# Batch 0's k in two kinds of load, a held queue, and another place for one product: linear attention into a SwiGLU block

## The chip, the cores and the metric

The kernel runs on one core of a Trainium2 chip. The time is that of the device in microseconds, median of three runs. A core has engines that run side by side: TensorE (PE) multiplies matrices and writes to PSUM, VectorE (DVE) and ScalarE (ACT) work element by element, GpSimd (POOL) and SyncE (SP) here mostly issue transfers (DMA). Each waits for the others by semaphores. In this kernel the instructions of an engine run in the order in which the program states them; nothing reorders them.

## The reference

Eight batches of eight heads, 576 positions, 64 elements a head. Attention without a softmax, its result as tokens into a gated block:

```python
def _attn_ref(q, k, v):
    def phi(x):
        return np.where(x > 0, x, np.exp(x) - 1.0) + 1.0
    q_p, k_p = (phi(q), phi(k))
    kv = np.einsum('bhsd,bhse->bhde', k_p, v)
    z = np.sum(k_p, axis=2)
    num = np.einsum('bhsd,bhde->bhse', q_p, kv)
    den = np.einsum('bhsd,bhd->bhs', q_p, z)[..., None] + 1e-06
    return (num / den).astype(np.float32)

def _moe_ref(x, w_gate, w_val, w_out):      # x: 4608 x 512, w_gate and w_val: 512 x 1536, w_out: 1536 x 512
    g = x @ w_gate
    silu = g * (1.0 / (1.0 + np.exp(-g)))
    val = x @ w_val
    return (silu * val @ w_out).astype(np.float32)
```

Since phi(x) = max(x, 0) + min(exp(x), 1), a phi costs one exp on ScalarE and a maximum, a minimum and an add on VectorE.

## The kernel before

The work goes in nine groups of 512 tokens. For each group, layer 1 is 12 blocks (`l1`, 8 products each), layer 2 is 4 blocks of 12 products. Attention for a batch is prepared while an earlier group is in the layers. Only batch 0 has nothing to hide behind: its attention is the head of the kernel. PSUM is four pairs of tiles (`pp4`), handed out in turn.

Loads: q of batch 0 comes in fp32 on SP's queue; everything else is issued by GpSimd and becomes fp16 on the way.

```python
def ld(src, dst, b, lp):                    # half lp of a batch: 288 KB of fp16
    nc.gpsimd.dma_start(out=dst[b % NB][:, 2 * lp:2 * lp + 2, :], in_=...)

for h in (0, 2):                            # q32 in two halves
    nc.sync.dma_start(out=q32[:, h:h + 2, :], in_=...)
nc.gpsimd.iota(out=idx[:, :], ...)
ld2(k, kr, 0)                               # both halves of k, then of v
ld2(v, vr, 0)
ld_w1(0, 256, 0, 2)                         # w_gate and w_val, by columns and rows
ld_w1(0, 256, 2, 4)
ld_w1(256, 512)
# ... the other columns, batch 1's k and q, w_out, batch 1's v
```

The head of batch 0. `lp` is one half of the heads. `warm` is products whose result nobody reads, to fill TensorE's waits. q is turned by TensorE and gets its phi afterwards (`q_exp` on ScalarE, `q_phi` on VectorE). `zt` sums k's phi over positions, once for the maximum (`kp`) and once for the minimum (`ek`); `zr_copy` takes the sum from PSUM; `t_corners` with `Zr` gives the denominator; `lnrd` its inverse by a logarithm and an exp for each of two tiles; `kv_corner` gives k.v, `r_copy` takes it from PSUM; `t_corners` with `R` gives the numerator; `x_t` multiplies the two into xT, the input of layer 1.

```python
nc.vector.tensor_copy(**q_cast(0))
act(**q_cast(1))
nc.vector.tensor_copy(**q_cast(2))
nc.vector.tensor_copy(**q_cast(3))
warm(WARM[0])
q_one(qa); q_one(qb)
q_turn(0, qa)
q_exp(0, 0, qa); q_exp(0, 1, qa)
warm(WARM[1])
q_turn(1, qb)
q_exp(1, 0, qb)
exp_k(0, 0)
q_exp(1, 1, qb)
warm(WARM[2])
exp_k(0, 1)
q_phi(0, 0, qa); q_phi(0, 1, qa)
mx_k(0, 0)                                  # maximum of k, first half
q_phi(1, 0, qb)
mn_k(0, 0)                                  # minimum of its exp
mx_k(0, 1)
zt(0, 0, X[1], kp, True, False)
warm(WARM[3])
zt(0, 0, X[1], ek, False, True)
zr_copy(0, 0, X[1])
warm(WARM[4])
t_corners(0, Zr, 0, pp4[2])
lnrd(pp4[2], 0)
add_k(0, 0)
mn_k(0, 1)
zt(0, 1, Y[0], kp, True, False)
kv_corner(0, 0, kp, True, True)
r_copy(0, 0, 1, "VV")
zt(0, 1, Y[0], ek, False, True)
zr_copy(0, 1, Y[0])
q_phi(1, 1, qb)
warm(WARM[5], ps=X[0])
t_corners(0, R, 0, X)
x_t(0, 0, X)
kv_corner(0, 1, kp, True, False)
t_corners(0, Zr, 1, Y)
lnrd(Y, 1)
# ... k.v with ek, R, then layer 1 by chunks of xT: l1_mm
```

Batch 1 is prepared in layer 2 of group 0, in two pairs, `dz` and `cq`. `den` writes a denominator into a pair and takes its logarithms, `cq` first. Before, k.v of batch 1 is written over `dz`.

```python
def p1_open():
    b1p["z"] = kvp[1] = pair()
    ring.pop()
    b1p["q"] = pair()
    ring.pop()

# in layer2_0:  cq, dz = b1p["q"], b1p["z"]
def s0():
    exp_q(1, 0); exp_q(1, 1); exp_k(1, 1)
    mx_p(0); mn_q(1, 0); add_p(0)           # phi of q, then of k's second half
    mx_p(1); mn_q(1, 1); add_p(1)
    mn_k(1, 1); add_k(1, 1)
# s1: turn(cq), q of batch 1 turned; s2: position 8 and z
def s4():
    den(1, cq)
    den(0, dz)
    for i in range(4):
        act(rd[i // 2][:, i % 2, :], lnt[i][:, :], AF.Exp, scale=-1.0)
# ...
s4()
for t in range(4):
    if t == 2:
        for lp in range(2):
            kv_corner(1, lp, kp, True, True)
        r_copy(1, 0, 2, "VV")
    if t == 3:
        nx(0, dz)                           # numerator and x_t, into dz, then into cq
        nx(1, cq)
    for fb in range(FO, FB):
        l2_mm(0, t, fb)
    # ...
```

Of the kernel before, what the change touches and what calls it, by code (L numbers as in the profile page):

```python
# [7 lines left out]
FP32 = mybir.dt.float32  # L8
# [5 lines left out]
P = 128  # L14
# [3 lines left out]
def kernel(  # L18
# [10 lines left out]
    nc = tc.nc  # L29

    B, H, S, D = q.shape
# [4 lines left out]
    J = S // C  # L36
# [3 lines left out]
    EPS = 1e-6  # L40
    SC = 4096.0
    NB = 3
    WARM = (4, 2, 5, 4, 2, 1)

    sb = ctx.enter_context(tc.tile_pool(name="sb", bufs=1))
    pp = ctx.enter_context(tc.tile_pool(name="ps", bufs=1, space=bass.MemoryType.PSUM))
# [2 lines left out]
    def many(shape, dt, name, n=2):  # L49
        return [sb.tile(shape, dt, name=f"{name}_{i}") for i in range(n)]  # L50

    kr = many([P, HL, J * D], FP16, "kr", NB)
    qr = many([P, HL, J * D], FP16, "qr", NB)
    vr = many([P, HL, J * D], FP16, "vr", NB)
    ek = many([P, 2, J, 2 * D], FP16, "ek")
    eq = many([P, HL, J * D], FP16, "eq")
    kp = many([P, 2, J, 2 * D], FP16, "kp")
    qp = many([P, 2, J, 2 * D], FP16, "qp")
    qT = many([P, 2, J, 2, C], FP16, "qT")
    R = many([P, 2, 2, D], FP16, "R", 3)  # L60
# [2 lines left out]
    rd = many([P, 2, 512], FP16, "rd")  # L63

    q32 = sb.tile([P, HL, J * D], FP32, name="q32")
    lnt = many([P, 512], FP32, "lnt", 4)
    prod = sb.tile([P, J, 2 * D], FP16, name="prod")
    den = sb.tile([P, 2, J * 2], FP32, name="den")
# [16 lines left out]
    gate = sb.tile([P, 1], FP16, name="gate")  # L85
# [7 lines left out]
    def pair(p=None):  # L93
        i = 0 if p is None else [x is p for x in ring].index(True)
        p = ring.pop(i)
        ring.append(p)
        return p
# [4 lines left out]
    def ld(src, dst, b, lp):  # L102
        nc.gpsimd.dma_start(out=dst[b % NB][:, 2 * lp:2 * lp + 2, :],  # L103
                            in_=src[b].rearrange("(l a) (c j) d -> (a c) l (j d)", a=2, j=J)[:, 2 * lp:2 * lp + 2, :])

    def ld2(src, dst, b):
        ld(src, dst, b, 0)
        ld(src, dst, b, 1)

    def ld_w1(f0, f1, c0=0, c1=4):  # L110
        for (src, dst) in ((moe_w_gate, wg), (moe_w_val, wv)):
            nc.gpsimd.dma_start(out=dst[:, c0:c1, f0:f1],
                                in_=src[P * c0:P * c1, f0:f1].rearrange("(c p) f -> p c f", p=P))

    def ld_w2(f0, f1):
        nc.gpsimd.dma_start(out=wo[:, f0:f1, :],
                            in_=moe_w_out[P * f0:P * f1, :].rearrange("(c p) f -> p c f", p=P))

    def act(out, in_, func=AF.Copy, scale=1.0, bias=0.0):
        nc.scalar.activation(out=out, in_=in_, func=func, bias=bias, scale=scale)  # L120

    def warm(n, w=512, ps=None):
        for _ in range(n):
            nc.tensor.matmul(out=(ps or pp4[1][1])[:, 512 - w:512], lhsT=ones[:, :],  # L124
                             rhs=ones[:, 0:1].to_broadcast([P, w]), start=True, stop=True)

    def hs(lp):
        return slice(2 * lp, 2 * lp + 2)

    def jl(t, b, lp):  # L130
        return t[b % 2][:, lp, :, :].rearrange("p j (l d) -> p l j d", d=D)

    def lj(t, b, lp):
        return t[b % NB][:, hs(lp), :].rearrange("p l (j d) -> p l j d", d=D)

    def exp_k(b, lp):
        act(jl(ek, b, lp), lj(kr, b, lp), AF.Exp)
# [4 lines left out]
    def mx_k(b, lp):  # L142
        nc.vector.tensor_scalar(out=jl(kp, b, lp), in0=lj(kr, b, lp), scalar1=0.0, scalar2=None, op0=ALU.max)  # L143

    def mn_k(b, lp):
        a = ek[b % 2][:, lp, :, :]
        nc.vector.tensor_scalar(out=a, in0=a, scalar1=1.0, scalar2=None, op0=ALU.min)  # L147
# [29 lines left out]
    kvp = {}  # L177
# [17 lines left out]
    def r_copy(b, l0, l1, engs):  # L195
        for hh in range(2):
            src = kvp[b][hh][:, D * l0:D * l1].rearrange("p (l d) -> p l d", d=D)
            if engs[hh] == "A":
                act(R[b % 3][:, l0:l1, hh, :], src)
            else:  # L200
                nc.vector.tensor_copy(out=R[b % 3][:, l0:l1, hh, :], in_=src)  # L201
# [42 lines left out]
    def units(g):  # L244
        us = seq[U * g:U * g + U]
        res = []
        for i, (b, j) in enumerate(us):
            if res and res[-1][0] == b and res[-1][2] == j:
                res[-1][2] = j + 1
            else:  # L250
                res.append([b, j, j + 1, C * i])
        return us, res
# [3 lines left out]
    def corners(ps, W, b, lp, j0, j1, c0):  # L256
        for l2 in range(2):
            rows = slice(D * l2, D * l2 + D)
            for hh in range(2):
                nc.tensor.matmul(out=ps[l2][C * hh:C * hh + C, c0:c0 + C * (j1 - j0)],  # L260
                                 lhsT=W[rows, lp, hh, :], rhs=qt(b, lp, hh, j0, j1)[rows],
                                 start=True, stop=True)
# [75 lines left out]

    for h in (0, 2):
        nc.sync.dma_start(out=q32[:, h:h + 2, :],
                          in_=q[0].rearrange("(l a) (c j) d -> (a c) l (j d)", a=2, j=J)[:, h:h + 2, :])
    nc.gpsimd.iota(out=idx[:, :], pattern=[[-1, P]], base=0, channel_multiplier=1)
    ld2(k, kr, 0)
    ld2(v, vr, 0)
    ld_w1(0, 256, 0, 2)
    ld_w1(0, 256, 2, 4)
    ld_w1(256, 512)
    ld_w1(512, 768)  # L350
    ld_w1(768, 1024)
    ld(k, kr, 1, 0)
    ld_w1(1024, 1280)
    ld_w1(1280, 1536)
    ld(k, kr, 1, 1)
    ld_w2(0, 4)
    ld(q, qr, 1, 0)
    ld_w2(4, 5)
    ld(q, qr, 1, 1)
    ld_w2(5, 6)  # L360
    ld_w2(6, 8)
    ld_w2(8, 12)
    ld2(v, vr, 1)

    nc.scalar.preload_act_table_set("natural_log_exp_and_others")
    nc.vector.memset(ones[:, :], 1.0)
# [53 lines left out]
    def zt(b, lp, ps, t, first, last):  # L420
        for j in range(J):
            nc.tensor.matmul(out=ps[:, 0:2], lhsT=t[b % 2][:, lp, j, :], rhs=ob[:, 0:P:C],  # L422
                             start=(first and j == 0), stop=(last and j == J - 1))

    def zr_copy(b, lp, ps):
        nc.vector.tensor_scalar(out=Zr[b][:, lp, :, :], in0=ps[:, 0:2].unsqueeze(2).to_broadcast([P, 2, D]),
                                scalar1=1.0 / SC, scalar2=None, op0=ALU.mult)
# [13 lines left out]
    def t_corners(g, W, lp, ps):  # L441
        for (b, j0, j1, c0) in units(g)[1]:
            corners(ps, W[b], b, lp, j0, j1, c0)

    def q_one(pair_):
        for h in range(2):
            nc.tensor.matmul(out=pair_[h][:, :], lhsT=part[:, :], rhs=ones[:, 0:1].to_broadcast([P, 512]),
                             start=True, stop=False)

    def q_turn(lp, pair_):  # L450
        for j in range(J - 1):
            nc.tensor.matmul(out=pair_[j // 4][:, P * (j % 4):P * (j % 4) + P],
                             lhsT=qp[0][:, lp, j, :], rhs=id16[:, :],
                             start=False, stop=(j % 4 == 3))

    def q_half(lp, h):
        return qT[0][:, lp, 4 * h:4 * h + 4, :, :].rearrange("p j h c -> p (j h c)")

    def q_exp(lp, h, pair_):
        act(q_half(lp, h), pair_[h][:, :], AF.Exp, bias=m1[:, 0:1])  # L460

    def q_phi(lp, h, pair_):
        a = q_half(lp, h)
        nc.vector.scalar_tensor_tensor(out=a, in0=pair_[h][:, :], scalar=1.0, in1=a, op0=ALU.max, op1=ALU.min)  # L464

    kvp[0] = pp4[1]
    X = [pp4[0][0], pp4[3][0]]
    Y = [pp4[3][1], pp4[0][1]]
    qa, qb = pp4[2], pp4[0]

    def q_cast(h):
        return dict(out=qp[0][:, h // 2, 0:8, D * (h % 2):D * (h % 2) + D],
                    in_=q32[:, h, 0:8 * D].rearrange("p (j d) -> p j d", d=D))

    nc.vector.tensor_copy(**q_cast(0))
    act(**q_cast(1))
    nc.vector.tensor_copy(**q_cast(2))
    nc.vector.tensor_copy(**q_cast(3))
    warm(WARM[0])
    q_one(qa)  # L480
# [3 lines left out]
    q_exp(0, 1, qa)  # L484
    warm(WARM[1])
    q_turn(1, qb)
    q_exp(1, 0, qb)
    exp_k(0, 0)
    q_exp(1, 1, qb)
    warm(WARM[2])  # L490
    exp_k(0, 1)
    q_phi(0, 0, qa)
    q_phi(0, 1, qa)
    mx_k(0, 0)
    q_phi(1, 0, qb)
    mn_k(0, 0)
    mx_k(0, 1)
    zt(0, 0, X[1], kp, True, False)
    warm(WARM[3])
    zt(0, 0, X[1], ek, False, True)  # L500
    zr_copy(0, 0, X[1])
    warm(WARM[4])
    t_corners(0, Zr, 0, pp4[2])
    lnrd(pp4[2], 0)
    add_k(0, 0)
    mn_k(0, 1)
    zt(0, 1, Y[0], kp, True, False)
    kv_corner(0, 0, kp, True, True)
    r_copy(0, 0, 1, "VV")
    zt(0, 1, Y[0], ek, False, True)  # L510
    zr_copy(0, 1, Y[0])
    q_phi(1, 1, qb)
    warm(WARM[5], ps=X[0])
    t_corners(0, R, 0, X)
    x_t(0, 0, X)
    kv_corner(0, 1, kp, True, False)
    t_corners(0, Zr, 1, Y)
# [22 lines left out]
    b1p = {}  # L540

    def p1_open():
        b1p["z"] = kvp[1] = pair()
        ring.pop()
        b1p["q"] = pair()
        ring.pop()

    def p1_z():
# [240 lines left out]
```

## Time and profile before

| what | value |
|---|---|
| time, median of 3 | 312.38 us (312.25 to 312.63) |
| span of the profiled run | 310.9 us |
| TensorE busy | 305.7 us (98%) |
| VectorE busy | 204.6 us (66%) |
| ScalarE busy | 153.1 us (49%) |
| GpSimd's queue: moved, share of 16 engines | 18.29 MB, 37.7% |
| SP's queue: moved, share of 16 engines | 13.96 MB, 18.8% |
| time from issue to landing, k in GpSimd's queue (median of 16) | 8.7 us |

Busy time is the sum of an engine's instructions, and TensorE's includes the warming products. A line of a timeline gives start and duration in microseconds, the engine, the line of the program, the operation, what it writes and reads, the shape, and in brackets how long the engine was idle before and what ended that. In the chain of waits each piece is what the next one waited for, followed back from the end. MB of a casting load are counted in what it writes.

### The profile page before, as it was taken

The numbers are of one execution on the slowest core, as the hardware profiler recorded it, in microseconds if no ns is written. First come the engines' busy times: TensorE is split into PE (matmuls) and PEld (weight loads), VectorE is DVE, ScalarE is ACT, GpSimd is POOL, SyncE is SP. The second block draws the span as 40 slices with busy tenths as digits, with TensorE's granted clock in tenths as the row PEclk, the third lists the DMA queues.
The fourth block names the chain that finished last, engine by engine and source line by source line (L and its number), as shares of the span: only waits on it lengthen the run. The fifth ranks groups of instructions, "written<-read, shape, count | busy, mean of one in ns | idle before, by whom it ended". The sixth has DMA issues, their size and how long they took to land.

```text
span 310.9 us, 5597 instructions
## 1 busy us (share of the span) xinstructions
PE 305.7 (98%) x2222; PEld 142.7 (46%) x2222; DVE 204.6 (66%) x361; ACT 153.1 (49%) x231; POOL 48.7 (16%) x74
## 2 busy tenths in 40 slices
PE   8999999999999999999999999999999999999996
PEld 3444444444544454445444544444444444444443
DVE  4755878999599667977697849874991343234320
ACT  4965868539733845365535743475331333133311
POOL 8664444410000410032000500000000000000000
PEclk9999999999999999999999999999999999999999
DMA  8999999999512594229712890314022400140014
GB/s 216 196 197 199 205 206 236 235 206 148 113 27 39 87 188 129 40 41 175 188 28 51 119 244 3 76 36 103 0 51 60 101 1 1 36 100 1 2 33 101
DMA packets 41162, 32.80 MB, mean 106 GB/s; under 512 B 16560, under 2 KB 36144, under 8 KB 41136
## 3 DMA queue, kind: packets, MB, share of 16 engines
q0 software_dynamic: 20496, 18.29, 37.7%
q1 hardware_dynamic: 20496, 13.96, 18.8%
q8 instruction: 17, 0.28, 0.4%
q10 hardware_dynamic: 144, 0.20, 0.2%
q14 instruction: 9, 0.07, 0.1%
HBM read 37.75 MB, written 9.44 MB: 152 GB/s over the span
## 4 chain that ended last, share of the span: by engine, by line
PE 95%; DMA 2%; DVE 1%; ACT 1%; issue 0%; POOL 0%; POOLq 0%; ACTq 0%
PE pp L298 58%; PE pp L305 30%; PE pp L282 2%; DMA kr<-in_k_dram 2%; PE pp L260 2%; PE pp L185 2%; ACT lnt L120 1%; PE pp L124 0%; PE pp L422 0%; PE pp L212 0%; DVE qT L464 0%; PE pp L384 0%; DVE kp L143 0%; DVE R L201 0%; DVE osb L328 0%
## 5 line engine op out<-in xcount | busy, mean ns | idle before, releaser
L120 ACT ACTIVATE sil<-pp 128x512 f16<-128x512 f32 x108 | 63.4, 597 | 100.8 <-PE pp L298 98.0
L298 PE MATMUL pp<-xT,wg 128*128 128x512 f16 x416 | 106.8, 379 | 0.0
L298 PE MATMUL pp<-xT,wv 128*128 128x512 f16 x416 | 106.8, 379 | 0.0
L291 DVE SCALAR_TENSOR_TENSOR hT<-pp,sil 128x512 f16<-128x512 f32 x108 | 72.4, 681 | 48.0 <-PE pp L298 35.3
L305 PE MATMUL pp<-wo,hT 128*128 128x512 f16 (+2 forms) x444 | 97.0, 374 | 0.0
L305 PEld LDWEIGHTS <-hT 128*128 128x128 f16 x444 | 41.9, 98 | 48.7 <-issue 0.8
L298 PEld LDWEIGHTS <-wv 128*128 128x128 f16 x416 | 40.7, 98 | 49.1
L298 PEld LDWEIGHTS <-wg 128*128 128x128 f16 x416 | 40.7, 98 | 48.4
L328 DVE TENSOR_SCALAR osb<-pp 128x512 f32<-128x512 f32 (+1 forms) x19 | 12.6, 667 | 31.9 <-PE pp L305 27.5
L120 ACT ACTIVATE osb<-pp 128x512 f32<-128x512 f32 (+1 forms) x18 | 10.5, 586 | 33.3 <-PE pp L305 33.3
L120 ACT ACTIVATE ek<-kr 128x1152 f16<-128x1152 f16 x16 | 17.9, 1156 | 0.5 <-DMA kr<-in_k_dram 0.4
L120 ACT ACT_TABLE_LOAD x13 | 16.7, 1283 | 2.3 <-PE pp L298 2.1
L719 POOL COPY gate<-qT 128x1 f16<-128x1 f16 x4 | 1.3, 314 | 96.6 <-DMA qT<-qp 96.6
L120 ACT ACTIVATE eq<-qr 128x1152 f16<-128x1152 f16 x14 | 15.7, 1152 | 1.3 <-DMA qr<-in_q_dram 1.3
L229 DVE TENSOR_TENSOR qp<-qp,rden 128x1152 f16<-128x1152 f16 x12 | 16.2, 1347 | 0.0
L220 DVE TENSOR_REDUCE den<-prod 128x18 f32<-128x1152 f16 x12 | 16.1, 1342 | 0.0
L277 DVE TENSOR_SCALAR xT<-pp 128x512 f16<-128x512 f32 (+1 forms) x14 | 8.8, 668 | 6.7 <-PE pp L260 6.7
L103 POOL DMA_DIRECT2D vr<-in_v_dram x16 | 11.7, 729 | 9.8 <-DMA wo<-in_moe_w_out_dram 4.1
L103 POOL DMA_DIRECT2D kr<-in_k_dram x16 | 11.6, 723 | 6.2 <-ACT lnt L120 1.0
L159 DVE TENSOR_TENSOR kp<-ek,kp 128x1152 f16<-128x1152 f16 x15 | 11.4, 758 | 0.5
L147 DVE TENSOR_SCALAR ek<-ek 128x1152 f16<-128x1152 f16 x16 | 7.7, 482 | 5.1 <-ACT ek L120 5.0
L103 POOL DMA_DIRECT2D qr<-in_q_dram x14 | 10.2, 727 | 5.3 <-DMA qr<-in_q_dram 2.7
(86 smaller groups left out, 181.6 us busy)
## 6 DMA issues: line engine op xcount, KB each, us to landing
out_dram<-osb SPq DMA_DIRECT2D x70, 128.0 KB, 2.9
kr<-in_k_dram POOLq DMA_DIRECT2D x16, 288.0 KB, 8.7
vr<-in_v_dram POOLq DMA_DIRECT2D x16, 288.0 KB, 10.0
qr<-in_q_dram POOLq DMA_DIRECT2D x14, 288.0 KB, 11.5
wg<-in_moe_w_gate_dram POOLq DMA_DIRECT2D x5, 256.0 KB, 8.6
wv<-in_moe_w_val_dram POOLq DMA_DIRECT2D x5, 256.0 KB, 9.2
q<-in_q_dram SPq DMA_DIRECT2D x2, 576.0 KB, 4.0
wo<-in_moe_w_out_dram POOLq DMA_DIRECT2D x2, 512.0 KB, 11.9
```

The costliest lines, as they stand in the source:

```text
L103: nc.gpsimd.dma_start(out=dst[b % NB][:, 2 * lp:2 * lp + 2, :], in_=src[b].rearrange("(l a) (c j) d -> (a c) l (j d)", a=2, j=J)[:, 2 * lp ...
L120: nc.scalar.activation(out=out, in_=in_, func=func, bias=bias, scale=scale)
L147: nc.vector.tensor_scalar(out=a, in0=a, scalar1=1.0, scalar2=None, op0=ALU.min)
L159: nc.vector.tensor_tensor(out=a, in0=ek[b % 2][:, lp, :, :], in1=a, op=ALU.add)
L185: nc.tensor.matmul(out=ps[hh][D * l2:D * l2 + D, D * lp:D * lp + D], lhsT=t[b % 2][rows, lp, j, D * l2:D * l2 + D], rhs=vr[b % NB][rows, 2 ...
L220: nc.vector.tensor_reduce(out=den[:, c, :], in_=prod[:, :, :].rearrange("p j (l d) -> p (j l) d", d=D), axis=AX.X, op=ALU.add)
L229: nc.vector.tensor_tensor(out=qv, in0=qv, in1=rden[:, c, :].unsqueeze(2).to_broadcast([P, 2 * J, D]), op=ALU.mult)
L277: nc.vector.tensor_scalar(out=dst, in0=ps[l2][:, c0:], scalar1=1.0 / SC, scalar2=None, op0=ALU.mult)
L291: nc.vector.scalar_tensor_tensor(out=hT[g % 2][:, fb, :], in0=ps[1][:, :], scalar=SC, in1=s[:, :], op0=ALU.mult, op1=ALU.mult)
L298: nc.tensor.matmul(out=ps[h][:, :], lhsT=w[:, c, P * fb:P * fb + P], rhs=xT[g % 2][:, c, :], start=(c == 0), stop=(c == 3))
L305: nc.tensor.matmul(out=l2p[(g, t)][:, n0:n1], lhsT=hT[g % 2][:, fb, P * t:P * t + P], rhs=wo[:, fb, n0:n1], start=(fb == 0), stop=(fb == F ...
L328: nc.vector.tensor_scalar(out=o[:, n0:n1], in0=ps[:, n0:n1], scalar1=1.0 / SC, scalar2=None, op0=ALU.mult)
```

## The change

The first half of batch 0's k goes to SP's queue as fp32, behind q, so that it comes ahead of everything that GpSimd loads; exp and maximum of that half read the fp32 tile. GpSimd's queue starts only when q's first half is cast, by a copy of one element of the result, so that its transfers don't compete with q's. To state that copy after the cast, the block of helpers moves up in the text; the helpers are the same. The order of the head is redone for the new arrivals, and the numbers of warming products with it. And k.v of batch 1 goes into the pair `cq`, whose logarithms come first, in place of `dz`.

```diff
-    WARM = (4, 2, 5, 4, 2, 1)
+    WARM = (4, 2, 6, 1, 2, 1)
+    k32 = sb.tile([P, 2, J * D], FP32, name="k32")
     def lj(t, b, lp):
-        return t[b % NB][:, hs(lp), :].rearrange("p l (j d) -> p l j d", d=D)
+        src = k32 if t is kr and b == 0 and lp == 0 else t[b % NB][:, hs(lp), :]
+        return src[:, :, :].rearrange("p l (j d) -> p l j d", d=D)
-    for h in (0, 2):
-        nc.sync.dma_start(out=q32[:, h:h + 2, :], in_=q[0]...)
+    for (src, dst, h) in ((q, q32, 0), (q, q32, 2), (k, k32, 0)):
+        nc.sync.dma_start(out=dst[:, h:h + 2, :], in_=src[0]...)
     nc.gpsimd.iota(out=idx[:, :], ...)
-    ld2(k, kr, 0)
     # ... constants, helpers (moved up)
+    nc.vector.tensor_copy(**q_cast(0))
+    nc.gpsimd.tensor_copy(out=gate[:, :], in_=qp[0][:, 0, 7, 0:1])
+    ld(k, kr, 0, 1)
     ld2(v, vr, 0)
     # ... all other loads, as before
     q_turn(1, qb)
+    exp_k(0, 0)
     q_exp(1, 0, qb)
-    exp_k(0, 0)
     q_exp(1, 1, qb)
     # ...
     mx_k(0, 0)
+    mn_k(0, 0)
     q_phi(1, 0, qb)
-    mn_k(0, 0)
-    mx_k(0, 1)
     # ... zt, zr_copy, t_corners, lnrd of the first half
     add_k(0, 0)
-    mn_k(0, 1)
-    zt(0, 1, Y[0], kp, True, False)
+    mx_k(0, 1)
     kv_corner(0, 0, kp, True, True)
     r_copy(0, 0, 1, "VV")
+    mn_k(0, 1)
+    q_phi(1, 1, qb)
+    zt(0, 1, Y[0], kp, True, False)
+    warm(WARM[5], ps=X[0])
+    t_corners(0, R, 0, X)
     zt(0, 1, Y[0], ek, False, True)
     zr_copy(0, 1, Y[0])
-    q_phi(1, 1, qb)
-    warm(WARM[5], ps=X[0])
-    t_corners(0, R, 0, X)
     x_t(0, 0, X)
     # ...
-        b1p["z"] = kvp[1] = pair()
+        b1p["z"] = pair()
         ring.pop()
-        b1p["q"] = pair()
+        b1p["q"] = kvp[1] = pair()
```

More of the change, by code (lines that the diff above doesn't have):

```diff
@@ L337, in l2_out @@
         return o
-    for h in (0, 2):
-        nc.sync.dma_start(out=q32[:, h:h + 2, :],
-                          in_=q[0].rearrange("(l a) (c j) d -> (a c) l (j d)", a=2, j=J)[:, h:h + 2, :])
+    for (src, dst, h) in ((q, q32, 0), (q, q32, 2), (k, k32, 0)):
+        nc.sync.dma_start(out=dst[:, h:h + 2, :],
+                          in_=src[0].rearrange("(l a) (c j) d -> (a c) l (j d)", a=2, j=J)[:, h:h + 2, :])
     nc.gpsimd.iota(out=idx[:, :], pattern=[[-1, P]], base=0, channel_multiplier=1)
-    ld2(k, kr, 0)
[L346 to L363, printed above, removed]
     nc.scalar.preload_act_table_set("natural_log_exp_and_others")
@@ L475 @@
     nc.vector.tensor_copy(**q_cast(0))
+    nc.gpsimd.tensor_copy(out=gate[:, :], in_=qp[0][:, 0, 7, 0:1])
+    ld(k, kr, 0, 1)
+    ld2(v, vr, 0)
+    ld_w1(0, 256, 0, 2)
+    ld_w1(0, 256, 2, 4)
+    ld_w1(256, 512)
+    ld_w1(512, 768)
+    ld_w1(768, 1024)
+    ld(k, kr, 1, 0)
+    ld_w1(1024, 1280)
+    ld_w1(1280, 1536)
+    ld(k, kr, 1, 1)
+    ld_w2(0, 4)
+    ld(q, qr, 1, 0)
+    ld_w2(4, 5)
+    ld(q, qr, 1, 1)
+    ld_w2(5, 6)
+    ld_w2(6, 8)
+    ld_w2(8, 12)
+    ld2(v, vr, 1)
     act(**q_cast(1))
```

## The prediction

> **What bounds the kernel now.** I read four views of the profile of before, in this order: the chain of waits for where the end comes from; the timeline where that chain leaves TensorE; the DMA view of the first 20 us; and the times to landing of single transfers.
>
> The chain of waits (start, duration, what):
>
> ```profile
> 1.35 6.95 DMA kr<-in_k_dram
> ...
> 8.32 0.47 DVE kp L143
> ...
> 18.12 17.27 PE pp L298 x80
> 35.38 5.18 PE pp L305 x24
> ...
> 44.43 1.85 ACT lnt L120 x3
> ...
> 46.32 0.79 PE pp L185 x71
> ```
>
> From 18.12 us on, the chain is TensorE work piece after piece, with one break: at 44.43 to 46.27 us it runs over ScalarE's logarithms. Everything that the change touches lies before 53 us; the other 258 us are matrix products it doesn't alter. So the change can only move two things: the head (0 to 18 us), which starts with k's first half landing at 8.30, and that break.
>
> The timeline around both (start, duration, engine, line, what):
>
> ```profile
> 1.35 1.54 POOL L103 DMA_DIRECT2D kr<-in_k_dram  x2 [0.29 <-issue]
> ...
> 4.34 0.43 DVE L475 CAST qp<-q 128x512 f16<-128x512 f32 x1 [2.37 <-DMA q<-in_q_dram]
> ...
> 8.32 0.46 DVE L143 TENSOR_SCALAR kp<-kr 128x1152 f16<-128x1152 f16 x1 [0.42 <-DMA kr<-in_k_dram]
> ...
> 9.96 1.15 ACT L120 ACTIVATE ek<-kr 128x1152 f16<-128x1152 f16 x1
> ...
> 13.11 1.45 DVE L435 SCALAR_TENSOR_TENSOR xT<-pp,rd 128x512 f16<-128x512 f32 x2
> ...
> 38.12 1.17 ACT L120 ACTIVATE eq<-qr 128x1152 f16<-128x1152 f16 x1 [0.48 <-DMA qr<-in_q_dram]
> ...
> 43.39 0.64 PE L260 MATMUL pp<-qT,Zr 64*64 64x64 f16 x16
> ...
> 45.79 0.21 PE L185 MATMUL pp<-vr,kp 64*64 64x64 f16 x1
> ...
> 46.32 0.79 PE L185 MATMUL pp<-vr,kp 64*64 64x64 f16 x71 [0.32 <-ACT lnt L120]
> ```
>
> The reader is to see three things. K is issued at 1.35 and used at 8.32. Batch 1's exp of q at 38.12 waited for a transfer. And k.v of batch 1 began at 45.79, stopped, and went on at 46.32.
>
> The DMA view of the first 20 us (GB/s in 40 slices of 0.5 us):
>
> ```profile
> GB/s 0 0 0 46 180 378 419 396 406 389 270 191 194 194 198 194 194 207 207 198 212 198 168 183 183 188 194 193 198 198 220 188 185 191 202 191 197 199 194 197
> ...
> q0 software_dynamic: 4518, 2.87, 99.0%
> q1 hardware_dynamic: 544, 1.18, 16.3%
> ```
>
> SP's fp32 load of q moves at some 400 GB/s; then GpSimd's casting loads move at some 195, counted in fp16 bytes, which is 390 GB/s of fp32 read. There is no gap from 2.5 us on, and the same view of 20 to 50 us stays near 205. The loads are one saturated stream until past 50 us, so every landing in it is a sum of bytes ahead of it, and a hole anywhere shifts all that follow. From the issues' times to landing: q's halves land at 4.33 and 5.79, k's at 8.30 and 9.74, v's at 11.2 and 12.65, first wv part at 13.97 (first used 14.15), second wv block 18.1 (used 18.82), batch 1's second half of q at 38.1 (used 38.12).
>
> [...] counting packets by queue, GpSimd's k, issued at 1.35, moves its first packet at 4.8, just as SP's q runs out (q's last packets are at 5.3). [...] After the idle spells of before I count 1.3 us to the first packet, and 2.1 to 2.3 us to the full rate (issues at 105.02, 137.78 and 171.28). [...] 1152 fp16 elements in 0.46 us, 512 fp32 ones in 0.43.
>
> **The change, part by part.**
>
> 1. The first half of k in fp32 on SP's queue. It follows q's 1.18 MB directly: 0.59 MB at 400 GB/s is 1.47 us, so its data ends at 5.3 + 1.47 = 6.8. Q's second half landed 0.5 us after its last packet (5.3 to 5.79), so k lands at 7.25 in place of 8.30: 1.05 us earlier.
>
> 2. Its first use. The maximum of k reads fp32. [...] VectorE has two q_phi before it (6.63 to 7.9), so it runs 7.9 to 8.65. Exp of k goes ahead of q's exp, at 7.25 to 8.4 (before 8.32 to 9.48). The min follows at 8.65 to 9.1 (9.52 to 9.98 before). But now q_phi(1,0) stands between the min and the copy of z, and ends only at 9.75 (q's exp, moved back, ends 9.05). So the copy of z starts near 9.8, not 10.46: of 1.05 us some 0.65 are left.
>
> 3. GpSimd's queue waits for q's first cast, ending 4.34 + 0.43 = 4.77. In the later periods the gate copy's start and the next issue are 0.54 us apart (104.48 and 105.02), so the first issue is at about 5.35, 4 us later than now. One transfer of 0.3 MB fp16 less is ahead in that queue. The first landing after an idle spell came 4.0 to 4.4 us after its issue (288 KB, same three places). So k's second half lands at 9.4 to 9.8: as before or slightly earlier. V's first half should follow at 11.0 to 11.4, against 11.2.
>
> 4. The stream. It reaches its full rate about 2.1 us after the issue, at 7.45; SP's data ends at 6.8. The hole is 0.65 us, less some 0.1 us worth of packets in the ramp[...]. Check by sums: before, GpSimd's stream flows from 5.05; after, from 7.45 but with one transfer less (1.53 us at 0.19 MB/us): 7.45 - 1.53 - 5.05 = 0.87. I take 0.7 us later for every landing from the weights on.
>
> 5. The rest of the head. The new order puts the maximum and minimum of k's second half, the copies of R and q_phi(1,1) ahead of the first xT product. From the z copy at 9.8: add to 10.6, maximum to 11.0; k.v waits for v (11.0 to 11.4) and takes 0.45; copies of R to 12.0; min 0.45, q_phi 0.6, z copy 0.25: xT starts at about 13.3, against 13.11. If v lands by 10.8 it is 12.8. So the 0.65 us mostly end in the wait for v; and the first product needs wv, due at 13.97 + 0.3 to 0.7. I expect the start of layer 1 within 0.4 us of now, either way.
>
> 6. Further on. Layer 1 of group 0 has 0.7 us to spare at its second wv block, 1.3 later; the shift of 0.7 just fits. Batch 1's q has nothing to spare: its exp waits for the landing, and the chain exp, min, add, transposes, copies, den ends in the products at 43.39, which TensorE reaches with 0.1 us to spare. So whatever the head gains is lost by 43.4, and the lateness of the stream shows: +0.6 us.
>
> 7. K.v of batch 1 goes to the pair whose logarithms are the first two of four, done by 45.05, before TensorE gets there at 45.8. The stretch from 45.79 to 47.10 (1.31 us) shrinks to the 0.78 us of 72 products: -0.53 us. The R copies then end before the products that need them; v of batch 1 lands at 45.5, or 46.2 if late, and its second half is needed 0.36 us into the work. Later, the exp of batch 2's q is bound by its landing (52.3), but the pair that waits for Silu behind it has 0.95 us to spare, and VectorE, full from 55 to 80, has some 0.5 us: the gain reaches the end.
>
> 8. Two warming products fewer (18 to 16), 0.21 us each, all in time when TensorE waits: nothing.
>
> Sum: +0.6 - 0.53, near +0.1; with the hole at half of that, -0.25.
>
> **Rivals.**
>
> Rival A, the head's gain reaches the end: the stream has no hole[...], and landings after 14 us are unchanged. For it: the author's own order, which expects v early. Against: the exp at 38.12 waits for its landing even now. It would give -0.5 from the break and at most -0.2 from the head: 311.6 to 311.9.
>
> Rival B, the first GpSimd transfer takes its 3.4 us to the first packet (1.35 to 4.8 before) whether or not SP's queue is busy: flow from 8.8, stream later by 2 us. Then the first wv is 1.8 us late and the head with it: +1.3 to +1.6, 313.7 to 314.0. For it: the number of the start itself. Against: the first packet came just as q ran out, and 1.3 us elsewhere.
>
> Rival C, k.v's new place only trades waits: the second pair's product now waits on R's copies. Against: those copies feed both products anyway. It would take away the 0.5: 312.9.
>
> **Range and chances.** My own sum is +0.1, rival A -0.6, rival B +1.4. Weighted 5 to 4 to 2 this is near +0.1; a change tuned by order speaks a little for A, so I say 312.3, 8 in 10 within 311.2 to 313.8. All of these are within 2% (6.2 us) of 312.38: faster 0.01, same 0.98, slower 0.01.
>
> **What would show it.** The fp32 k lands near 7.25 and the maximum takes about 0.76. GpSimd's first load is issued near 5.35, with the DMA row dipping between 6.8 and 7.5. Batch 1's exp of q starts at 38.5 to 39.0. The products at 43.39 come later, and k.v of batch 1 runs without a stop. I am wrong if the stream doesn't dip (A), or dips for over 1.5 us (B), or if layer 1 starts over 0.5 us earlier and keeps that past 43 us.

## The result, and the profile after

| | median | runs | lowest to highest |
|---|---|---|---|
| before | 312.49 us | 6 | 312.25 to 312.67 |
| after | 313.87 us | 6 | 313.65 to 315.32 |

The ratio is 1.0058, with a 95% interval of 1.0035 to 1.0081. The kernel became 1.4 us slower: outside the predicted range by 0.07 us, and on the side that I thought the less likely. The prediction's sum was +0.1.

The chain of waits of the kernel after, cut at 50 us (start, duration, what):

```profile
4.34 0.44 DVE qp L458
...
4.83 0.19 POOL gate L459
5.02 0.76 POOL kr L104
5.78 6.20 DMA vr<-in_v_dram
...
12.02 0.67 PE pp L187 x30
...
21.32 17.27 PE pp L300 x80
38.59 5.18 PE pp L307 x24
...
47.23 1.83 PE pp L307 x8
49.06 0.73 PE pp L187 x72
```

Before, the chain of the head started with k's issue and went over phi of k. Now the cast of q releases the queue, the queue loads v, and v's landing at 11.98 releases TensorE. K, for which the change was made, is not in the chain at all. The block of 80 products of layer 1 starts at 21.32 and took its 17.27 us before as well, but from 18.12. So 3.2 us are lost by 21 us, and the break at 44 us is gone: k.v is one piece of 72.

The timeline of after (start, duration, engine, line, what, and the idle time before it):

```profile
4.34 0.43 DVE L458 CAST qp<-q 128x512 f16<-128x512 f32 x1 [2.36 <-DMA q<-in_q_dram]
...
4.95 0.83 POOL L104 DMA_DIRECT2D kr<-in_k_dram  x1
...
8.03 0.76 DVE L145 TENSOR_SCALAR kp<-k 128x1152 f16<-128x1152 f32 x1
...
9.23 0.72 DVE L149 TENSOR_SCALAR ek<-ek 128x1152 f16<-128x1152 f16 x1 [0.43 <-ACT ek L121]
...
10.46 0.27 DVE L409 TENSOR_SCALAR Zr<-pp 128x128 f16<-128x128 f32 x1
...
12.02 0.67 PE L187 MATMUL pp<-vr,kp 64*64 64x64 f16 x36 [0.82 <-DMA vr<-in_v_dram]
...
15.85 0.61 PE L284 MATMUL pp<-xT,wg 128*128 128x512 f16 x1
...
39.67 2.22 ACT L121 ACTIVATE eq<-qr 128x1152 f16<-128x1152 f16 x2
...
48.99 0.80 PE L187 MATMUL pp<-vr,kp 64*64 64x64 f16 x72
```

and three lines of before to set beside it:

```profile
9.52 0.46 DVE L147 TENSOR_SCALAR ek<-ek 128x1152 f16<-128x1152 f16 x1
...
10.46 0.29 DVE L426 TENSOR_SCALAR Zr<-pp 128x128 f16<-128x128 f32 x1
...
11.47 0.48 PE L185 MATMUL pp<-vr,kp 64*64 64x64 f16 x36
```

Three things are to be seen. The copy of z starts at 10.46, which is exactly when it started before: nothing is left of the earlier k by then. The 36 products of k.v wait 0.82 us for v and take 0.67 us, not 0.48, and one product of 512 columns takes 0.61 us, where it took 0.38 to 0.39. TensorE has half its clock there, as the windows below show. And batch 1's two exps of q no longer wait for a landing; they are two in a row, because the layers themselves come later.

The DMA view of the first 20 us of after, in slices of 0.5 us:

```profile
GB/s 0 0 0 55 198 378 406 392 429 378 323 336 369 256 157 171 164 175 175 161 131 171 173 172 192 158 173 178 188 193 193 195 217 187 191 194 200 194 194 201
...
q0 software_dynamic: 3730, 2.32, 84.9%
q1 hardware_dynamic: 816, 1.77, 25.0%
```

The hole that I expected at 6.8 to 7.5 is not there. Counted by queue, GpSimd's first packet moves at 6.6 us, and SP's last one of k only at 7.7: in the three slices from 6.5 to 8.0 us SP moves 198, 65 and 14 GB/s, and GpSimd 58, 92 and 157. But from 7.0 us on the row does not come back to the 195 of before. It stays between 131 and 192 until about 14 us.

The same stretch of after by windows (length, busy time of PE, PEld, DVE, ACT and POOL with the numbers of instructions, granted clock, DMA share, GB/s):

```profile
6.00:8.00 2.00, 1.37 (x13) 0.84 (x13) 1.94 (x4) 0.82 (x2) 2.00 (x4) 1.00 0.99 238
8.00:10.00 2.00, 1.36 (x14) 0.45 (x13) 1.53 (x3) 1.97 (x3) 2.00 (x3) 1.00 1.20 169
10.00:12.00 2.00, 1.20 (x15) 0.56 (x16) 1.77 (x4) 1.82 (x3) 2.00 (x3) 1.00 1.06 162
12.00:14.00 2.00, 1.98 (x51) 1.04 (x51) 1.27 (x4) 1.94 (x4) 1.16 (x3) 0.52 1.33 175
14.00:16.00 2.00, 2.00 (x90) 1.65 (x87) 1.58 (x5) 0.70 (x2) 1.72 (x3) 0.50 1.44 192
16.00:18.00 2.00, 2.00 (x8) 0.44 (x6) 0.32 (x2) 1.94 (x4) 1.62 (x3) 0.50 1.45 197
```

and before:

```profile
6.00:8.00 2.00, 2.00 (x15) 0.85 (x14) 1.90 (x4) 1.62 (x3) 1.17 (x2) 1.00 1.18 195
8.00:10.00 2.00, 1.64 (x16) 0.55 (x13) 1.54 (x4) 1.68 (x3) 0.76 (x1) 1.00 1.20 202
10.00:12.00 2.00, 2.00 (x66) 1.26 (x66) 1.67 (x4) 1.83 (x4) 1.30 (x2) 1.00 1.29 190
```

TensorE is busy 1.37, 1.36 and 1.20 of each 2 us, where it was 2.00, 1.64 and 2.00. After that its granted clock is 0.52 and 0.50 for six microseconds. This doesn't happen in every run, and the profiled run is one of the longer ones (315.24 us in time). The table puts all 24 runs of the changed kernel, the six of the result and the 18 of the first experiment, by the mean clock that each run was granted:

| mean granted clock of the run | runs | median time |
|---|---|---|
| 1.000 | 5 | 313.56 us |
| 0.995 | 12 | 314.24 us |
| 0.988 or 0.989 | 7 | 315.56 us |

So there are two losses. One is there at full clock: 313.56 us is about 1 us over before. The other is a clock that falls, in some runs more than in others. The experiments had to say which part of the change makes each.

### The profile page after: what moved, and what is told of

Same layout as the page of the kernel before. It is cut to its first block, busy times and chain, and to the rows that moved or that the text cites. A ratio compares the mean times of both kernels' runs of the same rounds, so it can differ in the third digit from the quotient of the medians.

```text
span 313.5 us, 5592 instructions
## 1 busy us (share of the span) xinstructions
PE 306.9 (98%) x2220; PEld 142.7 (46%) x2220; DVE 204.8 (65%) x361; ACT 152.9 (49%) x231; POOL 48.4 (15%) x74
## 4 chain that ended last, share of the span: by engine, by line
PE 95%; DMA 3%; POOL 0%; DVE 0%; issue 0%
PE pp L300 57%; PE pp L307 30%; PE pp L284 3%; PE pp L262 2%; PE pp L187 2%; DMA vr<-in_v_dram 2%; DMA q<-in_q_dram 1%; POOL kr L104 0%; PE pp L405 0%; PE pp L214 0%; PE pp L367 0%; PE pp L125 0%; DVE qp L458 0%; DVE osb L330 0%; PE pp L556 0%; PE pp L385 0%
## 5 line engine op out<-in xcount | busy, mean ns | idle before, releaser
L121 ACT ACTIVATE osb<-pp 128x512 f32<-128x512 f32 (+1 forms) x18 | 10.5, 586 | 33.3 <-PE pp L307 33.3
L121 ACT ACTIVATE ek<-kr 128x1152 f16<-128x1152 f16 x15 | 16.8, 1156 | 0.2 <-DMA kr<-in_k_dram 0.2
L104 POOL DMA_DIRECT2D kr<-in_k_dram x15 | 10.8, 722 | 7.2 <-ACT sil L121 1.9
L161 DVE TENSOR_TENSOR kp<-ek,kp 128x1152 f16<-128x1152 f16 x15 | 11.4, 757 | 0.5
```

Source lines behind the costliest of these rows:

```text
L161: nc.vector.tensor_tensor(out=a, in0=ek[b % 2][:, lp, :, :], in1=a, op=ALU.add)
```

## The experiments

Ratios are against runs of the kernel before on the same chip, with their 95% intervals. None of the kernels leaves work out. The edits are to the kernel before or after, as each says.

### The changed kernel again, and k.v's place alone

The first is the changed kernel itself. The second is the kernel before with only the new place of k.v:

```diff
-        b1p["z"] = kvp[1] = pair()
+        b1p["z"] = pair()
         ring.pop()
-        b1p["q"] = pair()
+        b1p["q"] = kvp[1] = pair()
```

> The changed kernel as it is, for a second trace. In the first trace TensorE's granted clock was 0.5 from about 12 to 18 us (512 columns took 0.61 to 0.63 us, not 0.38), while four of the six timed runs had 0.995 to 1.0. If the lower clock is only an addition that some runs have, a run at clock 1.0 is still about 1.0 us of span above before (311.9 to 312.1 against 310.9), with v's first half landing near 12.0 and the start of layer 1 about 1.6 us later than before. If the lower clock is the whole cause, such a run would be at 310.9.

> The kernel before with one part of the change: batch 1's k.v goes into the pair whose logarithms come first. Theory: the stop in k.v at 45.79 to 46.32 goes, -0.5 us, 311.9 to 312.0. Rival (a trade of waits: the numerator's second pair then waits on the copies of R): no gain, 312.4 to 312.5.

The changed kernel again: 314.56 us, ratio 1.0062 (1.0041 to 1.0083), 18 runs. K.v's place alone: 312.04 us, ratio 0.9981 (0.9967 to 0.9996), 22 runs, the best time of any kernel in this study. From its chain of waits:

```profile
17.60 17.27 PE pp L298 x80
...
43.51 1.83 PE pp L305 x8
45.34 0.73 PE pp L185 x72
```

The 72 products run in one go, straight after layer 2's eight. This part of the change is a gain by itself, and everything else in it together costs 314.56 - 312.04 = 2.5 us.

### More warming products in the changed kernel

```diff
-    WARM = (4, 2, 6, 1, 2, 1)
+    WARM = (4, 2, 8, 3, 2, 1)
     # ... and ahead of k.v of batch 0's first half:
+    warm(4)
     kv_corner(0, 0, kp, True, True)
```

> The changed kernel with eight more warming products, all where TensorE waits in the trace: 8 for 6 before k's sum, 3 for 1 between its two parts, 4 new ones ahead of the first k.v. Theory (the clock falls where TensorE is idle over 6 to 12 us): no run with a clock under 0.995, the two slowest of six runs (315.3) don't come again, and the median is that of the changed kernel at full clock, 313.7 to 313.9. Rival (the lower clock has nothing to do with the waits): some runs at 315.3 as before. If the added products delay k.v, up to +0.3 us.

313.93 us, ratio 1.0045 (1.0029 to 1.0062), 22 runs, of which 21 have a mean clock of 0.999 or 1.000. By windows:

```profile
8.00:10.00 2.00, 2.00 (x18) 0.79 (x16) 1.40 (x3) 1.83 (x3) 2.00 (x3) 1.00 1.14 172
10.00:12.00 2.00, 1.94 (x20) 0.78 (x19) 1.90 (x5) 2.00 (x3) 2.00 (x3) 1.00 1.08 133
```

Products that nobody reads fill the waits, and the clock stays at 1.00. So in this kernel the fall of the clock comes from TensorE's waits (21 of 22 runs kept it, against 5 of 24 of after), and 314.56 - 313.93 = 0.6 us of the loss with it. (The median is still 0.4 us over the 313.56 of the changed kernel's own runs at full clock; no run shows why.) The rest stays: the stream is as slow as in after, 133 GB/s in its worst window. In this run it also reaches batch 1. In its chain of waits:

```profile
29.38 11.21 DMA qr<-in_q_dram
40.59 0.02 issue
40.61 1.17 ACT eq L121
```

Q of batch 1 lands at 40.59, 2.5 us later than the 38.1 of before, and the exp waits for it.

### The hold taken away, and shortened

Is it the hold of GpSimd's queue that makes v late? The first kernel is after without the gate's copy; the second lets the gate copy a constant that is ready at about 2 us, not q's cast.

```diff
-    nc.gpsimd.tensor_copy(out=gate[:, :], in_=qp[0][:, 0, 7, 0:1])     # first kernel: removed
+    nc.gpsimd.tensor_copy(out=gate[:, :], in_=ob[:, 127:128])          # second kernel
```

> The changed kernel without the copy that holds GpSimd's queue; nothing else. Theory (the held queue): GpSimd's first load is issued near 1.3 us again, its data follows SP's without a hole and at 190 GB/s or more from 7 to 12 us (160 to 175 with the gate), v's first half lands by 11.3 and not at 12.0, and the time falls by 1.0 us or more, to 311.9 to 312.8. Rival 1 (the loss is k's half in fp32 behind q and the new order on VectorE): within 0.3 us of the changed kernel, 313.5 to 314.1. Rival 2 (the gate was needed[...]): q's second half and k land over 0.5 us later than with the gate, and the time is 314 or more.

> The changed kernel, but GpSimd's queue is held only until VectorE's last memset (about 2.0 us, so its first load is issued near 2.2 us), just after SP has issued k (1.75 us), and not until q's first cast (4.8 us). Theory (transfers are served in the order in which they were issued, and the changed kernel loses by starting late): k in fp32 lands by 8.0, GpSimd's data follows without a hole at 190 GB/s, v's first half lands by 11.3, and the time is 311.5 to 312.5. Rival[...]: k in fp32 lands near 10, as without any hold (10.2), and the time is 315.5 or more.

No hold: 316.49 us, 1.0113 (1.0068 to 1.0158). Short hold: 314.93 us, 1.0081 (1.0063 to 1.0098). My theory fell: without the hold the kernel is slower still, though v's first half lands at about 11.0 us again (11.98 in after). So the hold is what makes v late; what goes wrong without it is k. The timeline of the kernel without it:

```profile
1.35 0.83 POOL L104 DMA_DIRECT2D kr<-in_k_dram  x1 [0.29 <-issue]
...
10.24 0.76 DVE L145 TENSOR_SCALAR kp<-k 128x1152 f16<-128x1152 f32 x1 [2.33 <-DMA k<-in_k_dram]
```

The fp32 half of k, issued at 1.75, lands at 10.21 without a hold, and the maximum of k at 10.24 waits for it; with the short hold it lands at 9.48, against about 8.0 in after. GpSimd's first packets move at 5.0 and 6.0, while SP's queue still has k to send, and from then on both queues move data side by side: without the hold SP moves 78 to 230 GB/s and GpSimd 83 to 147 in the slices from 5.5 to 8 us. The hold is what makes the fp32 k early. For q it does nothing that can be seen: the cast of its second half starts at 5.72 without the hold, at 5.80 in after and at 5.80 in before. Part of what these two kernels lose is again the clock: all six runs without a hold are at 0.989. But a low share of busy time does not make it fall in every run. The traced run with the short hold kept a full clock, though TensorE was busy less than in after:

```profile
6.00:8.00 2.00, 1.19 (x13) 0.79 (x13) 1.99 (x4) 0.69 (x2) 2.00 (x3) 1.00 1.08 254
8.00:10.00 2.00, 0.78 (x4) 0.17 (x2) 0.49 (x1) 0.49 (x1) 0.08 (x2) 1.00 1.17 215
10.00:12.00 2.00, 1.41 (x21) 0.68 (x21) 1.45 (x4) 2.00 (x4) 1.30 (x2) 1.00 1.23 203
```

### The hold alone, and the new loads in the old order

The hold on the old loads: both halves of k stay fp16 on GpSimd's queue, which is held until q's first cast; order and warming are those of before, and k.v has its new place. Beside it, the new loads and the hold, with order and warming of before. The first edit is to the kernel before with k.v in its new place, the second to the kernel after:

```diff
+    nc.gpsimd.tensor_copy(out=gate[:, :], in_=qp[0][:, 0, 7, 0:1])     # hold alone: after q's first cast,
+    ld2(k, kr, 0)                                                      # all of GpSimd's loads behind it
```

```diff
-    WARM = (4, 2, 6, 1, 2, 1)
+    WARM = (4, 2, 5, 4, 2, 1)                                          # new loads, old order:
     # ... exp_k, mn_k, mx_k, zt, zr_copy and q_phi of the head where they stood before
```

> The kernel before with k.v in its new place (312.04) and, of the loads, only the hold: both halves of k still come by GpSimd's queue, all of which waits for q's first cast. Old order. Theory (the hold is what costs): no data from 5.3 to about 6.6, then a slow stream of 160 to 175 GB/s until about 12 us, k's first half lands near 10.5, 2.2 us later than before; the time is 314.5 to 316. Rival (the slow stream comes from mixing k in fp32 with GpSimd's data): a hole of 1.5 us but then 190 GB/s and more, and 313.3 to 313.8.

> The changed kernel's loads and hold and k.v's new place, with the order and the warming products of before. Theory (the loads do it): as the changed kernel, 313.5 to 314.6, with the clock seldom under 0.995 since there are three more warming products between the parts of k's sum. Rival (the order does it): 312.0 to 312.6.

Hold alone: 315.22 us, 1.0088 (1.0074 to 1.0102). New loads in the old order: 313.53 us, 1.0033 (1.0021 to 1.0045), all five runs at full clock. The DMA view of the hold alone:

```profile
GB/s 0 0 0 51 147 396 373 415 415 396 166 0 12 85 191 196 194 210 187 141 99 138 175 182 171 171 184 181 176 184 193 195 194 196 219 180 197 194 196 199
```

SP's data ends at 5.3 us, and with nothing behind it the hole is open: 166, 0, 12, 85. The stream then comes to 190 and more for two microseconds and falls to 99 at 10 us. There is no fp32 k in this kernel, so the slow stretch is not from mixing with it. The chain of waits of the new loads in the old order:

```profile
6.45 7.42 DMA vr<-in_v_dram
13.87 0.04 issue
13.91 0.48 PE pp L187 x36
...
19.16 17.27 PE pp L300 x80
```

V's second half lands at 13.87 (12.65 before) and releases TensorE, and the 80 products start 19.16 - 17.60 = 1.56 us later than with k.v's place alone, at full clock. (Against the 18.12 of before it is 1.0: the head differs by half a microsecond from trace to trace.) In time it is 313.53 - 312.04 = 1.5 us. That is the cost of the new loads with their hold, without any fall of the clock. The hold alone costs 315.22 - 312.04 = 3.2, in four of its five runs with a clock of 0.995, though it has the order and the 18 warming products of before; the one run at full clock took 314.26, which makes it 2.2. The fp32 k fills the hole and gives back 0.7 of that at full clock (against that one run), and 1.7 between the medians.

The lateness can be read from the packets themselves. I take the time at which GpSimd's queue has moved as many bytes as before (and count the half of k that went to SP's queue as moved). At 14.5 us of before, after is 1.3 us late, its repeat 1.6, the new loads in the old order 1.5, and the hold alone 2.4; without a hold the queue is on time within 0.1. From there to 45 us these numbers stay the same within 0.1. So the prediction was right that a delay in this stream is passed on to all that follows, and the delays of the two kernels with the order of before, 1.5 and 2.4, are near what they lose at full clock, 1.5 and 2.2.

### The new order with the old loads, and fewer warming products

The new order and its warming on the old loads; the same with the warming of before; and k.v's place alone with two warming products fewer than before. All three have k.v in its new place. (The recorded expectation of the third counts three products fewer; its edit takes out two.)

```diff
-    WARM = (4, 2, 5, 4, 2, 1)
+    WARM = (4, 2, 6, 1, 2, 1)     # with the new order;  (4, 2, 5, 4, 2, 1) with it: the second
+    WARM = (4, 2, 4, 3, 2, 1)     # the third, in the old order
```

> New order, new numbers of warming products and k.v in its new place, but the loads of before: k by GpSimd's queue, nothing held. Theory (the order costs little by itself; the loads do it): 312.0 to 312.6 at full clock. Rival (the order costs: one more phi of q before the copy of z, and k's second minimum behind R): 312.8 to 313.5.

> New order and k.v's new place with the loads of before, as in the earlier run of the new order (312.29, where 3 of 21 runs had a clock of 0.988 to 0.995), but with the 18 warming products of before (four, not one, between the two parts of k's sum). Theory (the fewer warming products let the clock fall): no run under 0.998, median 312.0 to 312.3. Rival (the order lets it fall): again one run in seven or more under 0.996.

> The kernel before with k.v in its new place (312.04 by itself) and three warming products fewer (4 for 5, 3 for 4, 1 for 2), since in that kernel's chain of waits the warming products stand right before the sums of k. If they hold the head up: 311.5 to 311.9. If they are what keeps the clock at full: some runs with a clock of 0.988 to 0.995 and a median of 312.1 to 312.8.

New order with its warming: 312.29 us, 1.0000 (0.9987 to 1.0012). With the old warming: 312.37 us, 0.9993 (0.9986 to 0.9999). Old order, fewer warming products: 312.16 us, 0.9986 (0.9979 to 0.9994). On the old loads the order costs at most a few tenths: the medians are 0.2 and 0.3 us over that of k.v's place alone, and the intervals overlap. In the clock, with the new warming 3 of 21 runs fell to 0.995 or 0.988 (313.47, 313.55 and 315.35 us), with the old warming none of 21 fell below 0.998. Three against none is too few to call the warming products the cause. The third kernel, whose clock never went below 0.999, shows the other side: on the old loads and in the old order, two products fewer do no harm.

### What makes the stream slow

Two kernels on the slow stretch itself. The first puts a second hold into after: GpSimd issues k's second half and v, and the weights only after the minimum of k's first half. If issuing while data moves slows the data, the stream should be fast during the pause. The second has the old loads and order, k.v in its new place, and a hold to about 2 us: a later start that leaves no gap behind q.

```diff
     ld2(v, vr, 0)
     # ... after the minimum of k's first half:
+    nc.gpsimd.tensor_copy(out=gate[:, :], in_=ek[0][:, 0, 0, 0:1])
+    ld_w1(0, 256, 0, 2)           # and all that follows
```

```diff
+    nc.gpsimd.tensor_copy(out=gate[:, :], in_=ob[:, 127:128])
     ld2(k, kr, 0)                 # and all that follows
```

> The changed kernel with a second hold on GpSimd's queue: after k's second half and v are issued (to about 7.2 us), the weights wait for the minimum of k's first half (about 9.9 us). So between 7.2 and 10 us data moves while GpSimd issues nothing. Theory (issuing while the data moves is what slows the stream: 160 to 170 in place of 190 to 200 GB/s at 8 to 12 us): 190 GB/s or more from 8 to 10 us, few packets over 0.25 us there, v's first half lands by 11.4. Rival (the slow stretch has to do with starting late or with the data themselves): 145 to 175 GB/s from 8 to 10 us as in the changed kernel, v near 12. The time isn't what is asked: the weights come later still, so 315 to 318.

> The loads and order of before with k.v in its new place, and a hold on GpSimd's queue that ends at VectorE's last memset (about 2.0 us; first load issued near 2.2 us in place of 1.35), not at q's cast. Theory (a hold costs only when it lets SP's data run out: GpSimd's first packets come near 5 us in any case): full rate from 5.5 us on, k's first half lands at 8.0 to 8.6, 312.0 to 312.3. Rival (every issue later by 0.8 us makes every landing later by 0.8 us and slows the stream): k at 9.0 or later, 313 or more.

Second hold: 315.23 us, 1.0093 (1.0078 to 1.0109). GpSimd's timeline in it, and below it the DMA view:

```profile
5.79 1.45 POOL L104 DMA_DIRECT2D vr<-in_v_dram  x2
10.13 0.18 POOL L482 COPY gate<-ek 128x1 f16<-128x1 f16 x1 [2.90 <-DVE ek L149]
10.58 0.71 POOL L113 DMA_DIRECT2D wg<-in_moe_w_gate_dram  x1 [0.26 <-issue]
```

```profile
GB/s 0 0 0 51 194 401 392 410 392 406 277 249 313 281 212 161 164 187 166 143 145 136 189 184 176 130 165 175 177 172 124 109 131 147 164 169 167 160 176 182
```

From 7.24 to 10.58 GpSimd issues nothing, and in that time the row reads 161, 164, 187, 166, 143, 145. The theory fell. Short hold: 312.35 us, 0.9996 (0.9985 to 1.0007), and its DMA view:

```profile
GB/s 0 0 0 41 194 387 355 415 401 392 270 152 161 194 191 177 187 198 182 198 201 207 196 193 181 176 191 192 189 201 198 217 187 188 195 199 193 199 198 194
```

A hold to 2 us costs little: 312.35 against 312.04 (by the ratios, 0.9996 against 0.9981, nearer 0.5 us). Over all traces, the mean rate from 8 to 12 us splits the kernels in two. With the queue held to q's cast (after, its repeat, more warming, hold alone, old order, second hold) it is 165, 170, 152, 166, 158 and 164 GB/s. With no hold and the old loads (before, k.v's place, new order with either warming, fewer warming products) it is 196, 200, 197, 195 and 202; with the short hold 195. (The two kernels that send k in fp32 without the long hold have both queues in that window, so their 218 and 209 belong to neither.) Counting the trace's packets by queue at 9 to 10 us, GpSimd's queue moves:

```
kernel        KiB in 1 us  packets   mean length   longest
before            198        192       0.100 us     0.13 us
after             164        159       0.129 us     1.25 us
```

The median packet is 0.107 us in both. So the loss is a small number of very long packets, and fewer packets in all. What makes them long stays open: the mixing with the fp32 k is out (the hold alone has them), the issuing is out (the second hold has them). Nor is it that SP's queue has run dry: that is so in the hold alone (SP's last packet at 5.3 us, GpSimd's first at 6.4), but in the other five SP still sends when GpSimd starts (in after to 7.7, from 6.6). What the slow cases have in common is that GpSimd issued its first load at 4.9 us or later. With the fp32 k and the short hold it was issued at 2.16; the first packet moved at 6.0, only 0.6 us before that of after, and yet the stream was not slow: 203 GB/s from 10 to 12 us, when GpSimd's queue was alone. No run shows why a late issue should matter some microseconds later.

## Why the prediction was wrong, by its steps

The loss can be laid out along a chain of four kernels, from before to the changed kernel again. Each row is the step from one to the next, so the sum is right by construction; another order of the parts could share it out differently. The 313.53 was measured on another chip than the rest, where before took 312.42.

| part | from | us |
|---|---|---|
| k.v's new place | k.v's place alone, 312.04, against 312.46 | -0.4 |
| new loads with the hold, at full clock | old order with new loads, 313.53, against 312.04 | +1.5 |
| new order with fewer warming products, mostly by the clock | the changed kernel again, 314.56, against 313.53 | +1.0 |
| sum | 314.56 against 312.46 | +2.1 |

The third row is a matter of the clock: the three of those 18 runs at full clock took 313.29 to 313.56, no more than the old order with the new loads. The six runs of the result give +1.4; their spread over the clocks is similar, and their two runs at 0.995 (313.83 and 313.90) were hardly longer than those at full clock.

The step that failed is 4, the lateness of the stream: 0.7 us was forecast, and 1.3 to 1.6 came. Beside it stands the fall of the clock, which no step had; step 8 came nearest to it. In order:

- **Step 1, fp32 k at 7.25.** It landed at about 8.0. I took 400 GB/s to the end; the row of after reads 323, 336, 369 from 5 to 6.5 us, and from 6.6 us on GpSimd's packets moved beside the last of k, which lasted until 7.7. The gain of 1.05 us was 0.3, and even that is no more than single traces differ by: with the loads of before k's first half landed at 8.30 in before, at 7.76 with the new order, and at about 7.5 with fewer warming products.
- **Step 2, the first use.** Two sizes were right: 0.76 us for the maximum, and 1.16 us for the exp. (The 0.76 was an estimate of mine that the trace of before did not show. In after the fp32 maximum of 1152 elements took 0.76 us and the fp16 one 0.45.) They start at 8.03, 0.8 later than I said. The third was not: the minimum, which waits for the exp and not for the maximum, took 0.72 us in place of 0.46. So it ends at 9.95 (9.98 before), and the copy of z starts at 10.46 and not at 9.8: the 0.3 us of the earlier k went into the longer minimum. (In its repeat it took 0.72 again, in the second hold 0.46; no run shows why.)
- **Step 3, first issue at 5.35, k's second half at 9.4 to 9.8, v at 11.0 to 11.4.** The issue came at 4.95, 0.4 earlier; the packets at 6.6, 1.6 us after it, where the idle spells of before show 1.41 (I had counted 1.3); k at 10.5, v at 11.98. From before to after v lost 0.8 us, and TensorE waited 0.82 us for it. I had put v at worst 0.2 later.
- **Step 4, "I take 0.7 us later for every landing from the weights on".** There was no hole, but the first part of the delay was about as large as I said: counted by bytes, the stream of after was 0.6 us late at 8.9 us. What failed is that I let it end there: full rate 2.1 us after the issue and then 195 GB/s as before. In place of that the stream ran at 165 for the four microseconds from 8 to 12, which at 195 makes another 4 x 30 / 195 = 0.6 us, and the lateness grew to 1.3. Landings came 0.8 (v's first half) to 1.2 us later (v's second half in the kernel with the old order), and 2.5 us later for batch 1's q in the kernel with more warming. The term that I gave +0.6 in the sum measures +1.5.
- **Step 5, layer 1 within 0.4 us of now.** It was 1.0 to 1.6 us later at full clock (in the kernel with the old order), and 3.2 in the profiled run of after with the fallen clock. The wait for v was the right place to look; the landing was wrong.
- **Step 6, the lateness shows at 43 us.** It showed at the head. By the time of the exp of q the layers were late enough to hide it in after. In the kernel with the old order the exp does wait for its landing (at 39.39, 1.3 later than before), but TensorE's chain runs on; only in the kernel with more warming is that wait in the chain. The mechanism is real, but it was not the one that set this time.
- **Step 7, -0.53.** Right: one piece of 72 products in 0.80 us, -0.42 us by itself. It is in after as well, hidden by the rest.
- **Step 8, "Two warming products fewer: nothing".** It counted the products' own time and not what they are for. In the trace of after, TensorE was busy 60 to 69% of the time from 6 to 12 us, and then the clock was 0.5 for 6.8 us. The trace of the short hold with the fp32 k, less busy and at full clock, shows that the share alone does not settle it. It is not the fewer products alone, since the third of the warming kernels lost nothing; and the hold alone lost its clock in four of five runs with all 18 products. With the new loads and the new order, eight more products in TensorE's waits kept the clock at 0.999 or more in 21 of 22 runs. Whether the two products fewer had a part in it is not shown: no run has the new loads and the new order with 18. I wrote down that TensorE would wait for v, and did not ask what the wait does to the clock.

Rival A, no hole and all landings after 14 us unchanged, is out: no stretch was without packets, but the stream was 1.3 us late from there on. It stayed low for some seven microseconds, where I had named 1.5 as the sign of rival B. Rival C, the new place only trades waits, is out by k.v's place alone. Rival B named nearly the right time, 313.7 to 314.0, by the wrong mechanism, which is luck: it had the first packet 3.4 us after the issue, and it was 1.6. (In before the first packet moved at 5.0 and not at 4.8, so its own number should have been 3.6.) My range ended at 313.8 because I gave no weight to a slower stream or a slower clock. Neither was among my rivals.

## What to carry to other kernels

Holding a queue back so that another is served first had a price here in what the held queue brought later, even where no gap was left between the two: a hold to 2 us cost 0.3 to 0.5 us, a hold to q's cast 2 to 3, and with more data on the first queue still 1.5. When a change makes TensorE wait, count the filler products again: here repeated waits of half a microsecond to a microsecond cost 1 us in the median by the clock and 2 us in the worst runs. And when a change mixes parts, run each alone: the only gain here was the one line for k.v's place, which at 312.04 us beats both kernels.

## What the runs showed of the hardware

- **The casting stream that was issued late stayed slow.** In all six kernels where GpSimd's queue was held to q's cast, its first load issued at 4.9 to 5.0 us, it moved 152 to 170 GB/s from 8 to 12 us, against 195 to 202 where the first load was issued at 1.35 or 2.15 with the old loads. The median packet kept its 0.107 us; single ones took up to 1.25 us, against 0.13 at the same time before. The cause is open.
- **The wait from issue to first packet varied more than twofold.** GpSimd's first packet moved 3.6 to 3.8 us after an issue at 1.35 or 2.16 (at 5.0 in before, at 6.0 with the fp32 k and the short hold), 2.9 after the issue at 2.15 in the short hold on the old loads, and 1.5 to 1.8 after issues at 4.9 to 5.0 (6.6 in after, 6.4 in the hold alone). It is not just whether SP's queue is sending: in after it was, at 320 to 370 GB/s. What sets the wait is open. Where both queues had packets, both moved: without the hold SP moved 78 to 230 GB/s and GpSimd 83 to 147 from 5.5 to 8 us, and the fp32 half of k landed at 10.21 in place of 8.0.
- **The clock fell without a long gap, and for 3.4 or 6.8 us.** In the profiled run no wait of TensorE from 6 us to the fall at 12.1 was over 0.82 us; it was busy 1.2 to 1.4 of each 2 us for six microseconds. The same kernel kept the full clock in 5 of 24 runs, and lost 2 us by it in 7; and one traced run of another kernel was less busy and kept it. In the five traces where it fell in the head, the half clock lasted 6.8 us (after, its repeat, no hold) or 3.4 us (hold alone, second hold). Half of 3.4 us is 0.5% of the time, which is what a mean clock of 0.995 says, and 0.989 is about twice that.
